# Bringing attention's output back to tokens by DMA transpose instead of TensorE

## The chip, the cores and the metric

The kernel runs on one core of one Trainium2 chip. The metric is the device time of one execution in microseconds. Beside the plain times there is one execution with the hardware profiler on; all durations of instructions come from that one.

## The reference

Two blocks follow each other, all in 32-bit floats. Attention with 8 batches, 8 heads, 576 tokens and head dimension 64, in which each row of scores keeps its 32 largest; then an FNet layer over the 512 channels that the heads give together.

```python
scores = scale * np.matmul(q, k.transpose(0, 1, 3, 2))
kth = np.partition(scores, -top_k, axis=-1)[..., -top_k:-top_k + 1]
scores = np.where(scores >= kth, scores, -1000000000.0)
attn = np.exp(scores - np.max(scores, axis=-1, keepdims=True))
attn = attn / (np.sum(attn, axis=-1, keepdims=True) + 1e-09)
attn_out = np.matmul(attn, v)
...
x = attn_out.transpose(0, 2, 1, 3).reshape(B, S, H * D)
mixed = np.real(np.fft.fft(np.fft.fft(x, axis=1), axis=2))
u = x + mixed
un = (u - mean(u)) / np.sqrt(var(u) + 1e-06)
out = u + np.maximum(un @ w_ch1, 0.0) @ w_ch2
```

`w_ch1` has 512 x 2048 elements, `w_ch2` 2048 x 512.

## The kernel before

**Pairs, items and steps.** Two heads of a batch make a pair: 32 pairs, four for each batch. A pair is cut into 9 items of 128 rows of scores (`IN_PAIR`, L314): eight are 128 queries of one head, the one at position 4 holds the 64 left-over queries of both heads. So there are 288 items, and the main loop (L1468) emits one step for each: step i brings the scores of item i+3, the top-32 search of item i, the masking and exponential of item i-1, and so on. Each engine works through its own list in the order in which the loop emits it; engines meet at semaphores. In the text, "position" is an item's or step's place in its pair, 0 to 8.

**One item.** TensorE makes the scores, ScalarE copies them to SBUF; VectorE finds the 32 largest with four `MAX8` and three `MATCH_REPLACE8` (L406, L408), seven passes over 576 elements for each item; GpSimd turns the first and last of them into the two biases `nt` (`bounds`, L411); ScalarE and GpSimd mask (`mask`, L424), ScalarE takes the exponential with the sum of each row (`expo`, L434). The rows stay unnormalised; the sums go into `den`.

**P to key-major order.** The product with V needs P with keys on partitions. In batch 0, in pair 7 and in the last pair TensorE transposes it (`transposes`, L489). In the 26 other pairs (4 to 30 without 7, `by_dma`, L419) P goes by DMA: `plane` (L445) splits the 32-bit words into planes of low and high 16-bit halves with two ScalarE copies and SyncE writes them to DRAM (step i+2), and `turn` (L472) reads them back with a DMA transpose of 16-bit elements into `PT`, so that the halves come to lie beside each other again (step i+3). All these DMAs are issued on SyncE's queue, in order, with the loads of Q, K and V, the weight parts (`bring`, L884) and the stores of the output.

**The product and the way back to tokens.** A pair's queries form two chunks: chunk 0 has 320 (128, 128 and the 64), chunk 1 has 256. `attend` (L533) makes the output of a chunk in one PSUM bank `o`, with both heads' 64 channels on partitions and queries in the columns; in the 26 pairs it is emitted at the end of the step four after the chunk's last item (`chunk_at`, L1421). `attended` (L551) has ScalarE copy `o` to `xT` in SBUF and prepares the reciprocals `rd` of the row sums. `to_tokens` (L572), one step later, has TensorE transpose `xT` in 128-column pieces (three for chunk 0, two for chunk 1) into the same PSUM bank, and VectorE multiplies the result by `rd` into `x`, the batch's token-major activation: one instruction of 128x256 for each chunk, and one of 64x128 for chunk 0's tail. In batch 1, except for its last chunk, ScalarE does this multiplication in pieces of 64 columns (`normalise_on_act`, L600). `x` has two buffers, so a batch's chunks wait until the batch two before is stored (`written`).

**The FNet layer between.** When all chunks of batch b are in `x`, a plan made ahead (L1356) places the folding of x (GpSimd in the middle batches), the token and channel transforms on TensorE, the statistics and the transposition of u at fixed steps counted from `T0`. At the end the batch's MLP units join a queue (`mlp_units`, L930), and each step takes as many as its planned TensorE time leaves room for (`level`, L1441, spreads the queue up to the next batch's arrival). The last batch's MLP runs after the last step. GpSimd has places in a step: "pool0" is ahead of `bounds`; `some_sums` (L909) puts deferred sums of the MLP into what room is left.

Of the kernel before, what the change touches and what calls it, by code (L numbers as in the profile page):

```python
# [9 lines left out]
F32 = mybir.dt.float32  # L10
I32 = mybir.dt.int32
U32 = mybir.dt.uint32
U16 = mybir.dt.uint16
AF = mybir.ActivationFunctionType
ALU = mybir.AluOpType
# [4 lines left out]
P = 128  # L20
# [53 lines left out]
def kernel(  # L74
# [9 lines left out]
    nc = tc.nc  # L84
# [326 lines left out]
    def bounds(i):  # L411

        if i < N:
# [2 lines left out]
                out=Nt[i], in0=M8.pop(i)[:, 0:TOPK:TOPK - 1], in1=cc, op=ALU.mult  # L416
            )

    def by_dma(i):  # L419

        pair = i // PER_PAIR
        return NPB <= pair < NPAIR - 1 and pair != 2 * NPB - 1

    def mask(i, then=None):  # L424

# [125 lines left out]
    def attended(pair, ch, late):  # L551

        o, w = o_of.pop((pair, ch)), CW[ch]
        PT.pop((pair, ch))
        xT = attp.tile([P, CW[0]], F32, name=f"xT_{pair}_{ch}", tag="xT", bufs=4)
        nc.scalar.copy(out=xT[:, 0:w], in_=o[:, 0:w])
        xT_of[pair, ch] = xT
        den = den_t[pair % 3]
        if ch == 0:
            for h in range(2):  # L560
                nc.scalar.copy(
                    out=den[TH * h:TH * (h + 1), 5:6],
                    in_=den[TAIL + TH * h:TAIL + TH * (h + 1), 4:5],
                )
        c0, n = (0, 6) if ch == 0 else (6, 4)
        rd = small.tile([P, 6], F32, name=f"rd_{pair}_{ch}", tag="rd", bufs=6)

        nc.scalar.activation(out=rd[:, 0:n], in_=den[:, c0:c0 + n], func=AF.Copy, bias=1e-9)
        late.append(lambda: nc.vector.reciprocal(out=rd[:, 0:n], in_=rd[:, 0:n]))
        rd_of[pair, ch] = rd  # L570

    def to_tokens(pair, ch, at_once=True):  # L572

        b, hp = divmod(pair, NPB)
        if b not in x_of:
            x_of[b] = batp.tile([P, 5, DM], F32, name=f"x_{b}", tag="x", bufs=2)
        x = x_of[b]
        xT, rd = xT_of.pop((pair, ch)), rd_of.pop((pair, ch))
        shape, name = [P, 4, P], f"tpx_{pair}_{ch}"
        tp = ps_o.tile(shape, F32, name=name, tag="o") if at_once else bank(shape, name)  # L580
        for n, t in enumerate(CHUNKS[ch]):
            nc.tensor.transpose(tp[0:ROWS[t], n, :], xT[:, P * n:P * n + ROWS[t]], ident)
        cols = slice(P * hp, P * (hp + 1))

        def normalise():
            nc.vector.tensor_tensor(
                out=x[:, 2 * ch:2 * ch + 2, cols].rearrange("p t (e d) -> p t e d", e=2),
                in0=tp[:, 0:2, :].rearrange("p t (e d) -> p t e d", e=2),
                in1=rd[:, 0:4].rearrange("p (t e) -> p t e", e=2).to_broadcast([P, 2, 2, D]),
                op=ALU.mult,  # L590
            )
            if ch == 0:
                nc.vector.tensor_tensor(
                    out=x[0:TAIL, 4, cols].rearrange("p (e d) -> p e d", e=2),
                    in0=tp[0:TAIL, 2, :].rearrange("p (e d) -> p e d", e=2),
                    in1=rd[0:TAIL, 4:6].to_broadcast([TAIL, 2, D]),
                    op=ALU.mult,
                )

        def normalise_on_act():  # L600
            for n, t in enumerate(CHUNKS[ch]):
                r = slice(0, ROWS[t])
                for e in range(2):
                    hd = slice(D * e, D * (e + 1))
                    nc.scalar.mul(
                        out=x[r, t, cols][:, hd], in_=tp[r, n, hd],
                        mul=rd[r, 2 * n + e:2 * n + e + 1],
                    )


        if b == 1 and (hp, ch) != (NPB - 1, 1):
            at(now[0] + 1, "act", normalise_on_act)
        else:
            (late_now if at_once else late_next).append(normalise)
        return 0.14 * len(CHUNKS[ch])
# [662 lines left out]
    def at(step, where, fn, cost=0.0):  # L1278
        plan.setdefault((step, where), []).append(fn)
        costs[step] = costs.get(step, 0.0) + cost  # L1280
# [75 lines left out]
    for b in range(B):  # L1356
        end = PER_BATCH * (b + 1) - 1
        last = b == B - 1
        first, soon = b == 0, b == 1
        T0 = end + (2 if first else 3 if soon else 4 if last else 5)  # L1360
        if first:

            for op in fold_tails(b, nc.gpsimd):
                at(T0 - 1, "pool", op)

            def folds(b=b):
                for par, space in ((0, "own"), (1, "hT")):
                    for op in fold_ops(b, par, nc.vector, space):
                        op()
            at(T0, "dve", folds)  # L1370
            ft, fc = (T0 + 1, T0 + 1), T0 + 1
        elif soon:

            for n, op in enumerate(fold_tails(b, nc.gpsimd)):
                at(T0 - 2 + n, "pool0", op)
            for par in range(2):
                def folds(par=par, b=b, T0=T0):
                    for n, op in enumerate(fold_ops(b, par, nc.gpsimd)):
                        at(T0 + 1 + 3 * par + min(n, 2), "pool0", op)
# [24 lines left out]
        for n, t in enumerate((0, 1, 4, 2, 3)):  # L1404
            quick = first or last
            s = fc + (0 if first else n // 3 if last else n // 2)
            at(s, "pe2", lambda b=b, t=t, q=quick: dft_channels(b, t, q), 1.75)
            if not quick:
                at(s, "pool2", lambda b=b, t=t: add_mixed(b, t))
                at(s + 1, "dve", lambda b=b, t=t: stats(b, t))  # L1410
            at(s + (1 if quick else 2), "pe", lambda b=b, t=t: channels_first(b, t), 0.6)
            if first and t == 4:
                at(s + 1, "pe", lambda: (queue.extend(waiting), waiting.clear()) and 0.0)
        at(s + 1, "begin" if quick else "dve", lambda b=b: rsqrt(b))
        arrivals.append(s + (1 if quick else 2))
        at(arrivals[-1], "units", lambda b=b: (queue if b else waiting).extend(mlp_units(b)))
# [4 lines left out]
    def chunk_at(i):  # L1421

        for tile in (i - 4, i - 3, i - 2):
            r = tile % PER_PAIR
            if PER_BATCH <= tile < N and r in (4, 8):
                if i - tile == (4 if by_dma(tile) else 2 if tile == 2 * PER_BATCH - 1 else 3):
                    return tile // PER_PAIR, r // 8
        return None, None
# [20 lines left out]
    def run(i, where):  # L1449
        for fn in plan.pop((i, where), []):  # L1450
            fn()
# [13 lines left out]
    for op in top_ops(0, (0, 1)):  # L1465
        op()
    i, carry = 0, 0.0
    while i < N + 5 or plan or queue or sums:  # L1468
        now[0] = i
        run(i, "begin")  # L1470
        pair_of = i // PER_PAIR
# [19 lines left out]
        fixed += preps  # L1491

        tok = []

        if pending and pending[0][0] <= i and (
            i < 2 * PER_BATCH + 4 or chunk_at(i)[0] is None
        ):
            _, pp, pc = pending[0]
            if pp // NPB < 2 or pp // NPB - 2 in written:
                pending.pop(0)  # L1500
                tok.append(lambda: to_tokens(pp, pc, not short))
        if not short:
            fixed += tok
        for where in ("pe1", "pe2", "pe"):
# [19 lines left out]
        room = step_us - carry - fixed_cost(i)  # L1524
        cost, got = carry, 0.0
        turn(i - 3)
        if by_dma(i - 1):
            mask(i - 1)
        plane(i - 2, 0)
# [24 lines left out]
        if pair is not None:  # L1554
            cost += attend(pair, ch)
            attended(pair, ch, late_next)
            pending.append((i + 1, pair, ch))
        if i < N:
            if q_step:
                load_nat("k", pair_of + 1)  # L1560
# [67 lines left out]
```

## Time and profile before

| | |
|---|---|
| time, median of 3 runs | 1900.06 us (1898.37 to 1906.79) |
| the profiled execution | 1894.46 us, span 1892.7 us |
| mean granted TensorE clock | 0.953 |
| DMA traffic | 249.19 MB, 50.1% of the 16 engines' time |
| DMA transposes into `PT` | 130, on SyncE's queue |
| `MAX8` and `MATCH_REPLACE8` on VectorE (L406, L408) | 1482 us busy in all |
| steps on GpSimd's clock: first `nt` to last | 17.2 to 1699.1 us |

A row of the group view gives the instruction's line, engine and operation, the tile it writes and those it reads, shapes, the number of instructions, their busy time and mean duration, and then the idle time of the engine just before them with what ended it. Matmul times are those of a pipeline: a single one shows 273 ns where several in a row advance by some 140 ns.

### The profile page before, as it was taken

The page shows a single profiled execution, that of the slowest core. Times are in us where ns is not written, and L with a number is a line of the kernel's source. Part 1 is how long each engine was busy: PE and PEld are TensorE (multiplying, and loading weights), DVE is VectorE, ACT ScalarE, POOL GpSimd, SP SyncE. Part 2 cuts the span into 40 slices and gives each one's busy share as a digit, 9 for nine tenths or more (in the row PEclk, how much of TensorE's full clock was granted, in tenths as well). Part 3 has the DMA queues.
Part 4 walks back from the last instruction along what each step waited for, and adds up shares of the span by engine and source line. Part 5 has one row for each costly group of instructions (what it writes and reads, how often), then busy time and mean ns, then how long its engine had stood idle before and what let it go on. Part 6 is the DMA issues. An engine that isn't in the chain of part 4 may idle for free.

```text
span 1892.7 us, 27288 instructions
## 1 busy us (share of the span) xinstructions
PE 1720.7 (91%) x8134; PEld 1086.8 (57%) x8134; DVE 1580.9 (84%) x3301; ACT 1296.3 (68%) x3104; POOL 911.6 (48%) x1278
## 2 busy tenths in 40 slices
PE   5667699889899999999999999999999999999999
PEld 3344364365456654566456665666556655667677
DVE  7999999699899999997998998998999999862110
ACT  6878658577787777776777687767787778652100
POOL 4768643354745356354643565355544465341012
PEclk8878899899899999999999999999999999999999
DMA  5333026561567755585465854585456755430132
GB/s 166 106 93 108 20 63 167 155 158 32 137 154 191 179 132 131 135 208 141 123 157 135 228 123 124 146 218 145 124 147 172 198 129 144 122 116 6 50 101 80
DMA packets 521972, 249.19 MB, mean 132 GB/s; under 512 B 403680, under 2 KB 511841, under 8 KB 521825
## 3 DMA queue, kind: packets, MB, share of 16 engines
q1 hardware_dynamic: 521040, 247.24, 50.1%
q8 instruction: 65, 1.06, 0.2%
q14 instruction: 83, 0.67, 0.1%
q10 hardware_dynamic: 784, 0.21, 0.0%
HBM read 93.63 MB, written 84.74 MB: 94 GB/s over the span
## 4 chain that ended last, share of the span: by engine, by line
PE 64%; DVE 11%; ACT 9%; DMA 6%; POOL 5%; issue 3%; SPq 2%; POOLq 0%; DVEq 0%; ACTq 0%
PE hp L944 23%; PE cp L971 9%; PE o L542 8%; DVE m L406 5%; PE sp L382 5%; DVE wk L408 5%; PE yp L733 3%; PE cw L1141 3%; PE cv L1141 3%; PE cp L1010 3%; ACT wk L451 2%; POOL wk L430 2%; ACT wk L427 2%; DMA PT<-planes 2%; PE sp_t L352 2%
## 5 line engine op out<-in xcount | busy, mean ns | idle before, releaser
L430 POOL TENSOR_TENSOR wk<-S,wk 128x576 f32<-128x576 f32 x288 | 408.1, 1417 | 570.0 <-ACT wk L427 564.7
L406 DVE MAX8 m<-wk 128x8 f32<-128x576 f32 x864 | 626.7, 750 | 6.0
L944 PE MATMUL hp<-unT,w 128*128 128x256 f32 (+1 forms) x2048 | 533.9, 411 | 3.3 <-ACT hT L948 2.5
L944 PEld LDWEIGHTS hp<-unT,w 128*128 128x128 f32 x2048 | 378.0, 191 | 133.7 <-issue 29.9
L408 DVE MATCH_REPLACE8 wk<-m,wk 128x576 f32<-128x576 f32 x576 | 427.5, 742 | 0.0
L451 ACT COPY wk<-S 128x576 uint16<-128x576 uint16 x468 | 288.7, 666 | 0.1
L427 ACT ACTIVATE wk<-S,nt 128x576 f32<-128x576 f32 x288 | 222.3, 772 | 72.1 <-POOL nt L415 71.1
L971 PE MATMUL cp<-w,hT 128*128 128x512 f32 x512 | 247.8, 621 | 0.0
L406 DVE MAX8 m<-S 128x8 f32<-128x576 f32 x288 | 214.0, 743 | 34.5 <-ACT S L356 34.3
L542 PE MATMUL o<-PT,v 128*64 128x256 f32 (+3 forms) x1440 | 206.4, 430 | 24.9 <-DMA PT<-planes 16.7
L408 DVE MATCH_REPLACE8 wk<-m,S 128x576 f32<-128x576 f32 x288 | 213.6, 742 | 0.0
L438 ACT ACTIVATE S<-wk,nt 128x576 f32<-128x576 f32 x234 | 182.6, 781 | 43.8 <-POOL wk L430 42.6
L948 ACT ACTIVATE hT<-hp 128x320 f32<-128x320 f32 (+1 forms) x256 | 103.6, 410 | 151.5 <-PE hp L944 150.8
L382 PE MATMUL sp<-kT,qT 64*128 64x512 f32 (+1 forms) x528 | 180.3, 680 | 13.1 <-ACT means L1329 5.1
L542 PEld LDWEIGHTS o<-PT,v 128*64 128x64 f32 x1440 | 118.5, 158 | 110.5 <-issue 30.1
L971 PEld LDWEIGHTS cp<-w,hT 128*128 128x128 f32 x512 | 94.1, 197 | 110.4 <-issue 108.6
L385 ACT COPY S<-sp 128x512 f32<-128x512 f32 (+1 forms) x264 | 141.8, 587 | 18.1 <-PE sp L382 17.2
L1086 POOL TENSOR_TENSOR hT<-hT 128x512 f32<-128x512 f32 x64 | 81.4, 1275 | 99.3 <-ACT hT L948 86.4
L415 POOL TENSOR_TENSOR nt<-m,cc 128x2 f32<-128x2 f32 x288 | 58.6, 204 | 117.9 <-DVE m L406 113.9
L352 PE MATMUL sp_t<-kt,qT 128*128 128x128 f32 x320 | 71.9, 308 | 44.8 <-ACT S L374 27.4
L352 PEld LDWEIGHTS sp_t<-kt,qT 128*128 128x128 f32 x320 | 55.6, 197 | 99.2 <-ACT S L374 41.7
L1141 PE MATMUL cw<-w,hT 128*128 128x256 f32 x448 | 105.8, 383 | 0.9 <-issue 0.6
(160 smaller groups left out, 2130.4 us busy)
## 6 DMA issues: line engine op xcount, KB each, us to landing
planes<-wk SPq DMA_DIRECT2D x208, 288.0 KB
w<-w_parts SPq DMA_DIRECT2D x82, 512.0 KB
space<-in_moe_w_ch_dram SPq DMA_DIRECT2D x32, 512.0 KB
nat<-in_q_dram SPq DMA_DIRECT2D x128, 64.0 KB
v<-in_v_dram SPq DMA_DIRECT2D x128, 64.0 KB
out_dram<-x SPq DMA_DIRECT2D x32, 256.0 KB
nat<-in_k_dram SPq DMA_DIRECT2D x124, 64.0 KB
w_parts<-w_t SPq DMA_DIRECT2D x8, 512.0 KB
```

What stands on the lines that cost most here:

```text
L352: nc.tensor.matmul(sp[:, 0:P], lhsT=qT[:, q_end - P:q_end], rhs=kt_t, start=True, stop=True)
L382: nc.tensor.matmul(sp[r], lhsT=qT[hd, q_cols], rhs=kT[hd, :], start=True, stop=True)
L406: ops.append(lambda src=src, m8=m8: nc.vector.max(out=m8, in_=src))
L408: ops.append(lambda src=src, m8=m8: nc.vector.match_replace(w, m8, src, NEG))
L427: nc.scalar.activation(out=w, in_=Ssb[i], func=AF.Relu, scale=-FAR, bias=Nt[i][:, 1:2])
L430: nc.gpsimd.tensor_tensor(out=w, in0=Ssb[i], in1=w, op=ALU.subtract)
L438: nc.scalar.activation(out=Ssb[i] if by_dma(i) else w, in_=w, func=AF.Exp, bias=Nt.pop(i)[:, 0:1], accum_out=den_t[pair % 3][:, c:c + 1],)
L451: nc.scalar.copy(out=words[:, half, :], in_=src[:, half, :])
L542: nc.tensor.matmul(o[D * e:D * (e + 1), c0:c1], lhsT=vv[:, c, e, :], rhs=pt[:, NF if c == NF else (NF + 1) * e + c, c0:c1], start=(c == 0) ...
L944: nc.tensor.matmul(hp[:, 0:w], lhsT=w1[:, dt, P * it:P * (it + 1)], rhs=unT[:, dt, 0:w], start=(dt == 0), stop=(dt == NDT - 1),)
L971: nc.tensor.matmul(cp, lhsT=hT[:, it, P * n:P * (n + 1)], rhs=w2[:, it, :], start=(it == 0), stop=(it == NIT - 1),)
L1141: nc.tensor.matmul(dst, lhsT=h()[a][:, kc, :], rhs=rhs_of(kc), start=start and kc == 0, stop=kc == NK - 1, skip_group_check=True,)
```

## The change

In the 26 pairs whose P goes by DMA, the output of a chunk goes the same way. ScalarE copies `o` out of PSUM twice, as the low and the high 16-bit halves of its words (`words`, in the buffers of `xT`); SyncE writes the two planes to a DRAM tile `oplanes` (one DMA for the 256 columns of full tiles, for chunk 0 a second one for the 64 of the tail). Two steps later, instead of one, `to_tokens` issues a DMA transpose from there straight into `x` (chunk 0: a second one for the tail), in a new place "turn" of the step just behind the one of P. In the step after that GpSimd multiplies by `rd` in place, ahead of `bounds`. TensorE's transposes, the second use of the PSUM bank and the multiplication on VectorE (in batch 1 on ScalarE) go away for these pairs. `T0` of batches 2 to 6 moves from `end + 5` to `end + 7`, and with it everything planned from it.

```diff
+    def pair_by_dma(pair):
+        return NPB <= pair < NPAIR - 1 and pair != 2 * NPB - 1
     def by_dma(i):
-        pair = i // PER_PAIR
-        return NPB <= pair < NPAIR - 1 and pair != 2 * NPB - 1
+        return pair_by_dma(i // PER_PAIR)
...
         o, w = o_of.pop((pair, ch)), CW[ch]
         PT.pop((pair, ch))
-        xT = attp.tile([P, CW[0]], F32, name=f"xT_{pair}_{ch}", tag="xT", bufs=4)
-        nc.scalar.copy(out=xT[:, 0:w], in_=o[:, 0:w])
-        xT_of[pair, ch] = xT
+        if pair_by_dma(pair):
+            words = attp.tile([P, 2, CW[0]], U16, name=f"ow_{pair}_{ch}", tag="xT", bufs=4)
+            src = o[:, 0:w].bitcast(U16).rearrange("p (s h) -> p h s", h=2)
+            for half in range(2):
+                nc.scalar.copy(out=words[:, half, 0:w], in_=src[:, half, :])
+            to = xT_of[pair, ch] = dramp.tile(
+                [P, 2, CW[0]], U16, name=f"oplanes_{pair}_{ch}", tag="oplanes", bufs=6
+            )
+            nc.sync.dma_start(out=to[:, :, TAIL:], in_=words[:, :, 0:2 * P])
+            if ch == 0:
+                nc.sync.dma_start(out=to[:, :, 0:TAIL], in_=words[:, :, 2 * P:])
+        else:
...
         xT, rd = xT_of.pop((pair, ch)), rd_of.pop((pair, ch))
+        cols = slice(P * hp, P * (hp + 1))
+        if pair_by_dma(pair):
+            rows = xT.rearrange("p h s -> (p h) s")
+            nc.sync.dma_start_transpose(
+                out=x[:, 2 * ch:2 * ch + 2, cols].bitcast(U16), in_=rows[:, TAIL:]
+            )
+            if ch == 0:
+                nc.sync.dma_start_transpose(out=x[:, 4:5, cols].bitcast(U16), in_=rows[:, 0:P])
+            def normalise_in_place():
+                for t0, nt, n, r in ((2 * ch, 2, 0, P), (4, 1, 4, TAIL))[:2 - ch]:
+                    xs = x[0:r, t0:t0 + nt, cols].rearrange("p t (e d) -> p t e d", e=2)
+                    by = rd[0:r, n:n + 2 * nt].rearrange("p (t e) -> p t e", e=2)
+                    nc.gpsimd.tensor_tensor(
+                        out=xs, in0=xs, in1=by.to_broadcast([r, nt, 2, D]), op=ALU.mult
+                    )
+            at(now[0] + 1, "pool0", normalise_in_place)
+            return 0.0
...
-        T0 = end + (2 if first else 3 if soon else 4 if last else 5)
+        T0 = end + (2 if first else 3 if soon else 4 if last else 7)
...
-    while i < N + 5 or plan or queue or sums:
+    while i < N + 7 or plan or queue or sums:
...
         if pending and pending[0][0] <= i and (
-            i < 2 * PER_BATCH + 4 or chunk_at(i)[0] is None
+            i < 2 * PER_BATCH + 4 or chunk_at(i)[0] is None or pair_by_dma(pending[0][1])
         ):
...
-                tok.append(lambda: to_tokens(pp, pc, not short))
+                if not pair_by_dma(pp):
+                    tok.append(lambda: to_tokens(pp, pc, not short))
+                else:
+                    at(i, "turn", lambda: to_tokens(pp, pc))
...
         turn(i - 3)
+        run(i, "turn")
...
-            pending.append((i + 1, pair, ch))
+            pending.append((i + (2 if pair_by_dma(pair) else 1), pair, ch))
```

More of the change, by code (lines that the diff above doesn't have):

```diff
@@ L554, in attended @@
         PT.pop((pair, ch))
-        xT = attp.tile([P, CW[0]], F32, name=f"xT_{pair}_{ch}", tag="xT", bufs=4)
-        nc.scalar.copy(out=xT[:, 0:w], in_=o[:, 0:w])
-        xT_of[pair, ch] = xT
+        if pair_by_dma(pair):
[10 more added lines that the diff above has]
+        else:
+            xT = attp.tile([P, CW[0]], F32, name=f"xT_{pair}_{ch}", tag="xT", bufs=4)
+            nc.scalar.copy(out=xT[:, 0:w], in_=o[:, 0:w])
+            xT_of[pair, ch] = xT
         den = den_t[pair % 3]
@@ L582, in to_tokens @@
             nc.tensor.transpose(tp[0:ROWS[t], n, :], xT[:, P * n:P * n + ROWS[t]], ident)
-        cols = slice(P * hp, P * (hp + 1))
         def normalise():
```

## Prediction

> **What bounds the kernel now.** I read first the busy shares and the chain of work that ended last, for the engine to look at.
>
> ```profile
> PE 1720.7 (91%) x8134; PEld 1086.8 (57%) x8134; DVE 1580.9 (84%) x3301; ACT 1296.3 (68%) x3104; POOL 911.6 (48%) x1278
> ...
> PE 64%; DVE 11%; ACT 9%; DMA 6%; POOL 5%; issue 3%; SPq 2%; POOLq 0%; DVEq 0%; ACTq 0%
> ```
>
> TensorE (PE) is busiest and holds two thirds of the chain. That is a mean over stages, so next the busy time by stretch (stretch; length, PE busy, weight loads, DVE, ACT, POOL; clock, DMA share, GB/s).
>
> ```profile
> 500.00:700.00 200.00, 188.20 (x925) 120.46 (x922) 190.61 (x398) 158.63 (x379) 98.48 (x148) 0.97 0.65 163
> ...
> 910.00:1120.00 210.00, 201.97 (x974) 127.16 (x973) 194.65 (x406) 159.00 (x380) 104.71 (x155) 0.98 0.61 156
> 1120.00:1330.00 210.00, 202.02 (x963) 126.72 (x962) 190.50 (x398) 157.99 (x377) 104.56 (x155) 0.97 0.60 154
> 1330.00:1540.00 210.00, 204.23 (x1007) 129.43 (x1006) 195.82 (x409) 160.23 (x385) 106.21 (x157) 0.98 0.63 158
> ```
>
> From 910 us on, PE is 96 to 97% busy and DVE 91 to 93%: PE sets the pace there, DVE has some 15 us in 210 to spare. Before (500 to 700) PE has 94% and DVE 95%: either may set it. ACT (76%) and POOL (50%) have room everywhere. Third, what the way to tokens costs now (minimum/median/maximum ns).
>
> ```profile
> L582 PE MATMUL tpx<-ident,xT x160: 272/273/330, 51.5 to 1724.5; 128*128 128x128 f32 x128, 128*64 128x128 f32 x32
> L586 DVE TENSOR_TENSOR x<-tpx,rd x57: 382/425/426, 56.7 to 1724.8; 128x256 f32<-128x256 f32 x57
> L605 ACT ACTIVATE x<-tpx,rd x36: 305/316/349, 299.1 to 449.0; 128x64 f32<-128x64 f32 x28, 64x64 f32<-64x64 f32 x8
> L593 DVE TENSOR_TENSOR x<-tpx,rd x28: 273/273/275, 57.1 to 1698.5; 64x128 f32<-64x128 f32 x28
> ```
>
> **A, transposes off PE.** Five for each of 26 pairs, 130. In the timeline at 1000 us the three of a chunk 0 take 0.43 us from their start to the next product's start, the two of a chunk 1 at 1004 us 0.22 us: 0.65 a pair, 17 us in all, my lower bound. PE is marked busy with them for 0.49 + 0.38 us, 22.6 us in all, my upper bound. (That the PSUM bank is no longer used twice is worth nothing: products lie four or five steps apart, the second use is over in one.) I take 20, between. Of the 26 pairs 15 (pairs 16 to 30) lie where PE is the bound; I count 95% there. The other 11 lie where PE shares the bound; I count 55%. 20 x (15/26 x 0.95 + 11/26 x 0.55) = 15.6 us. Range 10 (lower bound, a third lost to idle PE) to 22.6.
>
> **B, normalising off DVE.** 23 pairs (batch 1 has it on ACT) x (2 x 0.42 + 0.27) = 25.6 us of DVE. Behind PE it lies hidden, also the 50.6 us in which DVE waited for `tpx`: DVE was ahead and only waited earlier than it would otherwise. In 455 to 860 us, 8 pairs, 8.9 us, DVE is a co-bound: a quarter, 2 us. Range 0 to 6.
>
> **C, ACT.** A second copy out of PSUM for each chunk. The trace has no 16-bit copy from PSUM; the rows nearest are the 32-bit copy of as many elements and the 16-bit strided copy in SBUF.
>
> ```profile
> L556 ACT COPY xT<-o 128x320 f32<-128x320 f32 x32 | 13.7, 428 | 53.5 <-PE o L542 53.5
> L556 ACT COPY xT<-o 128x256 f32<-128x256 f32 x32 | 11.9, 371 | 37.1 <-PE o L542 37.0
> ...
> L451 ACT COPY wk<-S 128x576 uint16<-128x576 uint16 x468 | 288.7, 666 | 0.1
> ...
> L1113 POOL TENSOR_TENSOR x<-x,ct 128x256 f32<-128x256 f32 x30 | 21.6, 729 | 4.5 <-ACT ct L1111 4.3
> ```
>
> By L556 it is 0.43 + 0.37 = 0.80 us a pair, 20.8 us; by L451's 1.16 ns per element 0.67, 17 us. I take 20.8. Batch 1 gives back 30 pieces of 0.32, 9.6 us. Net 11 us on an engine with 24% idle; the copies stand behind the chunk's product, ahead of the next step's work. At ACT's 9% of the chain it is 1 us. Without that cover, 11.
>
> **D, POOL.** 52 multiplications of 128x256 at L1113's 0.73 us and 26 tails of 64x128 (nearest: 128x128 at L629, 0.46) make 50 us. POOL idles 570 us ahead of its mask (the row of L430), waiting for ACT. But the place is ahead of `bounds`: queued behind the multiplication stands `nt`, for which ACT's mask waits. In the timeline POOL is idle 1.1 us between mask and `nt`, so 0.73 fits; chunk 0's 1.19 just does not. I take 1 us; if 1.2 us came on the path in 52 steps it were 62, which needs both PE and DVE without stock, so for the range 8.
>
> **E, SyncE and DMA.** Each pair adds three writes at L464's median 0.56 (1.7 us) and three transposes. A turn of 256 rows x 1152 columns is issued in 2.54 us (median of L484), of half as many rows in 1.26: in proportion, 256x256 takes 0.56, 256x128 0.28. No row has so small a transpose; the bounds are the plain issue's 0.44 and the turn's 1.26. I take 0.6, 0.6 and 0.5: 1.7 us. So 3.4 us a pair, 88 us on SyncE in all. What is queued behind? Loads, planes, turns; and PE's product waits for the last turn. That is tight: product 0 of a pair starts when the last turn has just landed.
>
> ```profile
> 991.40 0.60 SPq L980 DMA_DIRECT2D out_dram<-x  x1
> 997.86 0.54 SPq L464 DMA_DIRECT2D planes<-wk  x1
> 998.45 2.24 SPq L237 DMA_DIRECT2D nat<-in_q_dram  x4
> 1000.79 0.88 SPq L267 DMA_DIRECT2D nat<-in_q_dram  x2
> 1001.77 2.69 SPq L484 DMA_TRANSPOSE PT<-planes  x1
> 1004.56 0.58 SPq L466 DMA_DIRECT2D planes<-wk  x1
> ...
> 1008.38 1.29 SPq L484 DMA_TRANSPOSE PT<-planes  x1
> ```
>
> From 997.86 on the queue runs back to back into the planes of position 4 and its turn at 1008.38; the product starts at 1012.57. But it stood idle from 992.0 to 997.86, waiting for ACT's plane copies. The new transposes come just ahead of that: chunk 1's at position 5, chunk 0's at position 1, both positions without a turn of their own, so 0.6 to 1.1 us fall into this wait.
>
> ```profile
> SPq L464 <- ACT wk L451: 306.9, 104, 15.1
> SPq L484 <- DMA planes<-wk: 193.2, 109, 4.5
> ...
> PE o L542 <- DMA PT<-planes: 16.7, 7, 7.6
> PEld o L542 <- DMA PT<-planes: 9.2, 2, 8.5
> ```
>
> The writes add a wait on SyncE, for ACT's copies after the product. Behind it stands the turn of position 6 (after chunk 0) or 1 (after chunk 1), needed four steps later: about 1 us late, hidden. Not hidden: at a batch's start the chunks that waited for the store come on four successive steps, one perhaps ahead of the planes of position 4: 1 us, six times. The transposes move 26 x 256 x 640 elements more, an eighth of the turns' 26 x 1152 x 1152, at a DMA share of 0.6. I take 2 us; range 0 to 26 (1 us on each of 26 products 0).
>
> A rule speaks against the move. The Trainium skill, "VectorE: DVE Perf Modes", section "Rules for kernel authors", advises TensorE for a 128x128 transpose if the result may lie in PSUM, and the DMA crossbar otherwise; its section "The three transpose paths" gives 390 ns and 1309 ns for bf16. By these, five transposes in two halves would cost 13 us of transfer a pair in place of 2 us on PE, and if they stood on the path the kernel would lose some 290 us (an estimate from that page). The case's rows (0.14 us on PE, 2.5 us issue for a turn) agree on which is dearer; they say nothing against paying with a queue that waits.
>
> **F, the plan.** `T0` two steps later moves the MLP of batches 1 to 5 two steps back: batch 1's is spread over 44 steps instead of 42, and the debt is paid after batch 6's arrival. An MLP's products on PE come to (533.9 + 247.8 + 105.8 + 89.4 + 65.1)/8 = 130 us a batch (L944, L971, L1141 twice, L1010), 3.6 a step: 7.2 us of PE work leave the stretch 530 to 780 us, where PE isn't the only bound, and come back where it is. If 60% is saved there, 3 us are lost. Range 0 to 7.2. The two steps are what `x` comes later by: the transpose one step, the multiplication another; nothing reads `x` before `T0 - 2`.
>
> **Sum.** -15.6 - 2 + 1 + 1 + 2 + 3 = -10.6, about -11 us. The profiled execution (1894.46, of it 1892.7 span) lies 5.6 below the median of the runs shown, so it would come to 1883.5 and the median to 1900.06 - 11 = **1889 us**. Changes under 0.5% (9.5 us) count as none.
>
> **Rivals.**
> 1. PE's freed time becomes idle: DVE needs 7 x 0.745 = 5.2 us a step against 5.8, so it isn't the limit, but ACT and the landing of turns could be. Then a third of A (5 us) and nothing of B remain, less C to F's 7: about 1902, no change. For it: product 0 starts on a landing, so a PE that is earlier waits for it. Against: PE idles only 6 to 8 us in 210.
> 2. The turn becomes the bound (slower): SyncE's 3.4 us more per pair don't fit into the wait ahead of position 5's planes, the planes and turn of position 4 slip, and PE stands at each product 0. The spare there is about 1 us; it decides from a slip of (11 + 9.5)/26 = 0.8 us beyond it. At 1 us: 26 us instead of E's 2, and 5 us of A lost because PE, earlier, only waits: -11 + 24 + 5 = +18, 1918. For: 25.9 us of PE's waits are this one already. Against: the 306.9 us that SyncE waits for ACT.
> 3. POOL holds: the multiplication waits in order for its transpose's landing, with `nt` and the mask behind it. At 1.5 us in 26 of 52 steps +39 - 11, 1928. Against: the transpose is issued a whole step, 5.8 us, earlier.
>
> That the pairs don't take the new path is excluded by the code: the test is that of P's.
>
> **How the numbers follow.** Forecast 48%, rival 1 27%, rival 2 18%, rival 3 7%. The forecast's own range is 1873 (A at 22.6, B at 6, C to F near 1) to 1890. The whole: 1873 to 1918 leaves out 4% below and, above, half of rival 2 and nearly all of rival 3, some 15%. Faster 0.48, same 0.27, slower 0.25.
>
> **What would show it.** Right: 130 fewer PE transposes, PE's share in 910 to 1540 unchanged at 96% or more with shorter steps; POOL near 960 us, ACT near 1307, DVE near 1555; "PE o <- DMA PT" still near 26 us. Rival 1: PE's share falls by 1 to 2 points there. Rival 2: that wait grows over 50 us, and SyncE's wait for ACT shrinks. Rival 3: a wait of POOL's `x` for the new DMA, over 30 us. I am wrong if `T0` costs more than 7 us, seen as a tail after the last `nt` longer than today's 193 us by more than that.

## The result and the profile after

The changed kernel takes 1956.61 us, median of 4 runs (1954.99 to 1960.23); the kernel before took 1899.21 us (1893.26 to 1906.79, 4 runs) beside it. The ratio is 1.0303, 95% interval 1.0263 to 1.0343: 57 us slower, where some 11 us less were predicted and 1918 us was the upper end of the range.

The busy shares and the chain of waits, after:

```profile
PE 1723.6 (88%) x8004; PEld 1085.1 (56%) x8004; DVE 1568.3 (80%) x3232; ACT 1306.2 (67%) x3126; POOL 951.1 (49%) x1356
...
PE 52%; ACT 10%; DMA 10%; DVE 9%; POOL 8%; issue 6%; SPq 4%; POOLq 0%; DVEq 0%; ACTq 0%
```

The 130 transposes are gone from PE (8134 to 8004) and ACT and POOL moved as far as was forecast, DVE half as far; but PE is busy as long as before in a span that is 61 us longer (1953.9 us): 230 us of it are idle, where it was 172. In the chain PE went from 64 to 52% and DMA from 6 to 10%. The stretches of the middle (columns as in the prediction) say the same:

```profile
500.00:700.00 200.00, 175.66 (x842) 113.39 (x841) 181.59 (x373) 153.71 (x369) 94.72 (x147) 0.94 0.68 168
...
910.00:1120.00 210.00, 193.98 (x913) 119.24 (x912) 181.94 (x372) 154.89 (x373) 106.72 (x160) 0.98 0.66 160
1120.00:1330.00 210.00, 194.75 (x910) 121.43 (x911) 184.90 (x379) 155.76 (x371) 109.54 (x165) 0.98 0.67 165
1330.00:1540.00 210.00, 190.25 (x904) 118.62 (x904) 180.91 (x371) 153.39 (x368) 108.03 (x163) 0.97 0.65 158
```

From 910 us on PE is at 91 to 93% instead of 96 to 97%, and DVE at 86 to 88% instead of 91 to 93%: now no engine has a full stretch. What both wait for stands in the waits by engine and line (us in all, times, longest):

```profile
PE o L544 <- DMA PT<-planes: 58.1, 19, 8.6
...
PEld o L544 <- DMA PT<-planes: 23.0, 7, 6.2
...
POOL x L606 <- DMA x<-oplanes: 22.0, 14, 3.9
```

PE's wait for the turn of P has grown from 16.7 us to 58.1. POOL's new wait, 22.0 us in 14 places, is small. On SyncE's own queue, and then the new DMAs one by one (count: minimum/median/maximum ns of the issue, first and last start):

```profile
SPq L466 <- ACT wk L453: 211.4, 58, 14.9
SPq L486 <- DMA planes<-wk: 90.4, 68, 2.0
...
SPq L565 <- ACT rd L582: 73.5, 28, 8.5
...
SPq L565 <- ACT den L575: 68.3, 23, 7.2
...
SPq L596 <- DMA out_dram<-x: 6.8, 4, 1.9
```

```profile
L565 SPq DMA_DIRECT2D oplanes<-ow x52: 533/572/1111, 291.2 to 1728.1; - x52
L596 SPq DMA_TRANSPOSE x<-oplanes x52: 1192/1224/2203, 299.3 to 1733.0; - x52
L567 SPq DMA_DIRECT2D oplanes<-ow x26: 605/606/620, 291.8 to 1702.3; - x26
L600 SPq DMA_TRANSPOSE x<-oplanes x26: 1135/1236/2542, 300.5 to 1707.9; - x26
```

A transpose into `x` holds the queue for 1.22 to 1.24 us whether it is 256x256 or 256x128; 0.6 and 0.5 were assumed. With the writes (52 x 0.57 + 26 x 0.61 = 46 us) the new DMAs take 46 + 78 x 1.23 = 142 us of SyncE instead of the predicted 88. The time in which SyncE stood idle for ACT's planes and for their landing, 500 us before, is down to 302.

The place where this reaches PE is seen in the timeline, SyncE first, then PE (start, us, engine, line), in the second pair of batch 5:

```profile
1211.06 1.23 SPq L596 DMA_TRANSPOSE x<-oplanes  x1
1212.35 1.23 SPq L600 DMA_TRANSPOSE x<-oplanes  x1
1213.69 0.59 SPq L466 DMA_DIRECT2D planes<-wk  x1
1216.31 3.32 SPq L486 DMA_TRANSPOSE PT<-planes  x1
1219.68 1.26 SPq L596 DMA_TRANSPOSE x<-oplanes  x1
```

```profile
1221.95 4.53 PE L544 MATMUL o<-PT,v 128*64 128x256 f32 x20 [5.37 <-DMA PT<-planes]
```

A store issued at 1208.98 us frees `x`, and the chunks that waited for it are brought back on successive steps. SyncE holds the first of their transposes, and with it the queue, until the store has landed (the wait of `L596` for `out_dram` above: 6.8 us in four places, here 1.7). Two transposes stand ahead of the planes, the planes ahead of the turn, and the product of chunk 1 stands 5.4 us for it. From the issue of this store to that of the turn it is 7.3 us; in the kernel without the new DMAs (below) it is 3.6 us at the same place, 1173.52 to 1177.14, and this product doesn't wait. Then the granted clock (windows; the last three columns are clock, DMA share and GB/s):

```profile
1216.50:1221.90 5.40, 0.08 (x1) 0.00 (x0) 5.23 (x15) 3.94 (x11) 1.54 (x2) 0.93 0.84 136
1221.90:1225.30 3.40, 3.35 (x16) 1.95 (x18) 3.40 (x9) 0.00 (x0) 2.20 (x10) 0.50 0.57 145
1225.30:1228.70 3.40, 3.40 (x12) 1.15 (x9) 2.92 (x7) 2.17 (x6) 2.36 (x10) 0.61 0.33 111
1228.70:1232.10 3.40, 3.40 (x15) 2.37 (x14) 3.37 (x9) 1.79 (x4) 1.81 (x4) 1.00 0.97 196
```

After the gap PE runs at half clock for some 6 us (3.4 us at 0.50 and most of the next 3.4): the wait of 5.4 us costs about 3 us more behind it, half of those 6 (an estimate from these rows). That is a second price of every long wait, and the forecast had none.

### The profile page after: what moved, and what is told of

It is laid out like the page before. It is cut to its first block, busy times and chain, and to the rows that moved or that the text cites. A ratio compares the mean times of both kernels' runs of the same rounds, so it can differ in the third digit from the quotient of the medians.

```text
span 1953.9 us, 27252 instructions
## 1 busy us (share of the span) xinstructions
PE 1723.6 (88%) x8004; PEld 1085.1 (56%) x8004; DVE 1568.3 (80%) x3232; ACT 1306.2 (67%) x3126; POOL 951.1 (49%) x1356
## 4 chain that ended last, share of the span: by engine, by line
PE 52%; ACT 10%; DMA 10%; DVE 9%; POOL 8%; issue 6%; SPq 4%; POOLq 0%; DVEq 0%; ACTq 0%
PE hp L976 22%; PE o L544 7%; PE cp L1003 5%; DVE m L406 4%; PE sp L382 4%; DVE wk L408 4%; PE cw L1173 3%; DMA PT<-planes 3%; PE cv L1173 3%; POOL wk L432 3%; DMA planes<-wk 3%; DMA w<-w_parts 3%; ACT wk L429 2%; PE yp L765 2%; ACT wk L453 2%
## 5 line engine op out<-in xcount | busy, mean ns | idle before, releaser
L429 ACT ACTIVATE wk<-S,nt 128x576 f32<-128x576 f32 x288 | 222.4, 772 | 73.8 <-POOL nt L415 73.5
L544 PE MATMUL o<-PT,v 128*64 128x256 f32 (+3 forms) x1440 | 210.8, 440 | 61.9 <-DMA PT<-planes 58.1
L1003 PE MATMUL cp<-w,hT 128*128 128x512 f32 x512 | 242.2, 612 | 0.0
L352 PEld LDWEIGHTS sp_t<-kt,qT 128*128 128x128 f32 x320 | 55.8, 199 | 103.5 <-ACT S L374 41.8
L561 ACT COPY ow<-o 128x320 uint16<-128x320 uint16 (+1 forms) x104 | 36.3, 401 | 96.6 <-PE o L544 96.6
```

The costliest lines, as they stand in the source:

```text
L429: nc.scalar.activation(out=w, in_=Ssb[i], func=AF.Relu, scale=-FAR, bias=Nt[i][:, 1:2])
L544: nc.tensor.matmul(o[D * e:D * (e + 1), c0:c1], lhsT=vv[:, c, e, :], rhs=pt[:, NF if c == NF else (NF + 1) * e + c, c0:c1], start=(c == 0) ...
L1003: nc.tensor.matmul(cp, lhsT=hT[:, it, P * n:P * (n + 1)], rhs=w2[:, it, :], start=(it == 0), stop=(it == NIT - 1),)
```

## The experiments

Ratios are to the kernel before on the same chip, with 95% intervals; "+n us" is the ratio less one, times 1899 us.

**Which part costs the time.** Four kernels take the change apart. The kernel before with only the later `T0` (`t0_alone`):

```diff
-        T0 = end + (2 if first else 3 if soon else 4 if last else 5)
+        T0 = end + (2 if first else 3 if soon else 4 if last else 7)
...
-    while i < N + 5 or plan or queue or sums:
+    while i < N + 7 or plan or queue or sums:
```

> The kernel before with nothing but T0 of batches 2 to 6 at end + 7 (and the loop's end at N + 7). Theory S (SyncE's queue: 78 transposes at 1.2 us of issue and 78 writes that wait for ACT make the turns of P land late) expects the price of my term F alone, 1899 to 1906 us. Theory P (the plan: the folds and transforms now fall on worse positions of the pair, and the MLP comes late) expects most of the 57 us, over 1930.

1921.82 us, ratio 1.0141 (1.0125 to 1.0156): +27 us. And the kernel after with all of its change except the DMAs (`no_dma`; `x` then holds other numbers than attention's output, and that these take the same time is assumed, not shown):

```diff
-            to = xT_of[pair, ch] = dramp.tile(
...
-            nc.sync.dma_start(out=to[:, :, TAIL:], in_=words[:, :, 0:2 * P])
...
+            xT_of[pair, ch] = words
...
-            nc.sync.dma_start_transpose(
...
-                        out=xs, in0=xs, in1=by.to_broadcast([r, nt, 2, D]), op=ALU.mult
+                        out=xs, in0=src, in1=by.to_broadcast([r, nt, 2, D]), op=ALU.mult
```

> The changed kernel without its writes to DRAM and its transposes into x: ScalarE still copies both halves, GpSimd still multiplies, but constants by rd, so x does not hold attention's output. T0 is that of the changed kernel. Theory S expects the loss to be gone: 1885 to 1905 us. Theory P, and a theory L that puts the loss on ScalarE's second copy or on GpSimd's multiplication ahead of the biases, expect it to stay over 1935.

1897.26 us, ratio 1.0009 (0.9992 to 1.0025): +2 us. From here to the kernel after only the writes and transposes are added; the plan is the same step for step, also in the next two. The same kernel with the writes kept (`writes_only`):

> The changed kernel with its writes to DRAM but no transposes into x (GpSimd multiplies constants by rd, x does not hold attention's output). 1897.3 us without both, 1956 with both. If the reads' 1.2 us of issue on SyncE make the loss: 1900 to 1912. If the writes' waits for ScalarE make it: 1935 to 1955. Issuing the writes a step later changed nothing (1958.4), so I expect the former.

1913.14 us, 1.0088 (1.0065 to 1.0110): +17 us. And with the transposes kept, from planes in DRAM that are written once (`reads_only`):

> The changed kernel without its writes: the transposes into x read one fixed DRAM tile, written once at the start, so x does not hold attention's output. If the reads make the loss: 1940 to 1955. If reads and writes share it by their time on SyncE (96 to 46 us): about 1935. If the writes make it: 1900 to 1912.

1931.70 us, 1.0184 (1.0159 to 1.0208): +35 us. So the writes are worth 15 us over the kernel without DMAs, the transposes 33, both 56. The page and the waits of the kernel without the DMAs:

```profile
PE 1696.9 (90%) x8004; PEld 1074.5 (57%) x8004; DVE 1566.2 (83%) x3232; ACT 1303.0 (69%) x3126; POOL 949.3 (50%) x1356
```

```profile
PE o L544 <- DMA PT<-planes: 19.6, 7, 6.7
```

Its span is 1889.7 us; the kernel after's is 64 us longer (the profiled execution without the DMAs was the fastest of its ten, so this is more than the 56 of the ratios). PE's idle time is 193 against 230 us, and the wait for turns alone (19.6 to 58.1) is 38 us. The other 27 us are PE's busy time for the same 8004 instructions (1696.9 to 1723.6). Adding up the granted clock's half-rate stretches over PE's busy time gives a loss of 69 us without the DMAs and 87 with them, so 18 of the 27 are half clock; where the other 9 come from was not followed. With the transposes alone PE's wait for turns is 41.5 us; with the writes alone it is 17.6, no more than without any DMA, so the writes' 15 us come another way, and that was not followed either.

**Does it matter where on the queue they stand?** The new place "turn" moved from behind the turn to behind the planes of item i-2 (`reads_after_planes`):

```diff
         turn(i - 3)
-        run(i, "turn")
         if by_dma(i - 1):
             mask(i - 1)
         plane(i - 2, 0)
...
+        run(i, "turn")
```

> The changed kernel with its transposes into x issued behind the two planes of the step instead of ahead of them. Theory S, if the transposes' place ahead of the planes is what delays the turns: 1920 to 1945 us, and fewer products that wait for a turn (81 us of PE's waits on PT now). If the issue time counts wherever it stands: 1950 to 1960. Theory P: 1957.

1950.64 us, 1.0291 (1.0276 to 1.0306). The writes of `oplanes` issued one step later, where ACT's copies are long done:

```diff
-            nc.sync.dma_start(out=to[:, :, TAIL:], in_=words[:, :, 0:2 * P])
...
+            def write():
+                nc.sync.dma_start(out=to[:, :, TAIL:], in_=words[:, :, 0:2 * P])
...
+            at(now[0] + 1, "turn", write)
```

> The changed kernel with its writes of the planes of o issued one step later, behind the next step's turn, when ScalarE's copies are long done. Theory S, if SyncE's wait for ScalarE at those writes (about 142 us in sum) is what delays the turns: 1920 to 1945 us. If that wait only replaces other idle time of SyncE: 1950 to 1960. Theory P: 1957.

1958.42 us, 1.0330 (1.0314 to 1.0345). The 142 us in which SyncE stood for ACT at the writes fall to 24, its waits for planes and their landing rise from 302 to 402, and the time stays: that wait was idle time SyncE had anyway. Transposes behind the planes and only at the four positions that have no turn of their own, up to two chunks in one step (`reads_free`):

```diff
+            if pair_by_dma(pending[0][1]) and i % PER_PAIR not in (1, 3, 5, 8):
+                break
```

> The changed kernel with its transposes into x issued only at positions 1, 3, 5 and 8 of a pair, which have no turn of their own, behind the planes, two chunks at most at once. If the loss is that the transposes of waiting chunks push the planes and turns of positions 4 to 8: 1920 to 1940. If every microsecond on SyncE counts wherever it stands: 1948 to 1960.

1950.01 us, 1.0324 (1.0270 to 1.0378). PE's wait for turns is 41.8 us in both runs with the transposes moved, instead of 58.1. Of time hardly anything comes of it: by the ratios 2 us less and 4 us more than the kernel after, by the medians 6 and 7 us less. Pair by pair the wait changes its place: PE's gaps at chunk 1's products fall from 38.6 us to 15.4 and 19.3, those at chunk 0's rise from 21.8 to 29.8 and 29.3. So neither of these orders takes the loss away.

**Issue time or traffic?** Plain DMAs of 16 columns, DRAM to DRAM, in place of writes and transposes: two for each transpose, so SyncE is held about as long while almost nothing moves (`issue_only`).

```diff
-            nc.sync.dma_start_transpose(
...
+            for _ in range(4 if ch == 0 else 2):
+                nc.sync.dma_start(out=issue_to[:, :, 0:16], in_=fixed_planes[:, :, 0:16])
```

> Like the run with reads alone (1931.7 us), but each transpose into x is replaced by two small DMAs between DRAM tiles (8 KB each), about the same time of issue on SyncE and hardly any traffic; x is made of constants. 1897.3 us with nothing there. If issue time on SyncE makes the reads' 34 us: 1920 to 1935. If it is the transposes' traffic or GpSimd's wait for their landing: 1897 to 1910.

2027.26 us, 1.0716 (1.0673 to 1.0758). All of them write one DRAM tile, so that each waited for the one before: 195.5 us of waiting on the queue that the transposes don't have. The run is no measure of issue time alone; it shows that waits and issues together cost 134 us over the kernel without DMAs. With 24 tiles in turn instead (`issue_small`):

```diff
+                to = dramp.tile([P, 2, 16], U16, name=f"issue_to_{pair}_{ch}_{_}", tag="issue_to", bufs=24)
+                nc.sync.dma_start(out=to, in_=fixed_planes[:, :, 0:16])
```

> The run with two small DMAs in place of each transpose into x again, but each into a DRAM tile of its own (24 in turn), so that SyncE does not wait for the one before (195 us of such waits in that run). 156 issues of about 0.5 us, 80 us on SyncE, hardly any traffic; x is made of constants, T0 at end + 7. 1897.3 us without them. Theory Q (each microsecond that SyncE's queue is held costs some 0.35 to 0.45 us, whatever holds it: 0.35 with writes or reads alone, 0.41 with both, 0.45 with the waits) expects 1922 to 1935. Theory R (it is the transposes' own: traffic, landing, GpSimd's wait) expects 1897 to 1908.

1920.95 us, 1.0126 (1.0088 to 1.0164): +22 us over the kernel without DMAs (15 to 29 by this run's interval). The DMAs in the view of their tile:

```profile
L592 SPq DMA_DIRECT2D issue_to<-oplanes_fixed x156: 487/605/1454, 298.9 to 1700.1; - x156
```

156 x 0.605 = 94 us of issue, as much as the transposes' 96, cost 22 us where the transposes cost 33. Some two thirds of the transposes' price is thus time on the queue, by the interval from under a half to nearly nine tenths. PE's wait for turns is 33.0 us here. From 500 to 1540 us the medians from issue to landing hardly change between the kernels before and after: 4.68 and 4.74 us for a turn, 2.67 and 2.70 for planes. So the remaining third does not show as slower transfers of these; it stays open.

The other way round, load taken off the queue: the loads of V issued by GpSimd, in the kernel after (`v_pool_after`) and in the kernel before (`v_pool_before`).

```diff
-            load_full(v_of[pair], v, pair)
+            q_of_v = nc.sync if pair == 0 else nc.gpsimd
...
+                for h in range(2):
+                    load_half(v_of[pair], v, pair, e, h, q_of_v)
```

> The changed kernel with the loads of V (6 DMAs a pair, 0.5 us of issue each, 101 us of SyncE in all) issued from GpSimd's queue. Theory Q expects 35 to 45 us less than the 1956 of the changed kernel, 1911 to 1925, less what GpSimd pays for issuing. Theory R expects 1950 or more.

2007.31 us, 1.0591 (1.0555 to 1.0627).

> The kernel before with the loads of V issued from GpSimd's queue. If SyncE's queue already limits the kernel before in the same measure (theory Q without a threshold): 1860 to 1880. If the queue limits only past what it carries there: 1890 to 1905.

1954.96 us, 1.0311 (1.0275 to 1.0348). The edit costs 55 us in the one and 59 in the other, for a reason of its own: in the kernel before with this edit

```profile
L237 POOL DMA_DIRECT2D v<-in_v_dram x124: 720/736/946, 55.5 to 1694.8; - x124
```

an issue takes 0.74 us of GpSimd itself, its busy time rises from 911.6 to 1043.2 us, and ACT's wait for `nt` from 71.1 to 163.5. So the price of a relieved queue can't be read from these times. One thing they do show: in `v_pool_after` SyncE's issues add up to 912 us, against 1016 in the kernel after and 868 without the new DMAs, yet PE waits 62.4 us for turns, as much as before the edit, and 34.2 us at chunk 1's products. The loads of V stand at position 7, those turns at position 2: time taken off the queue in one place is not given back in another.

Last, the weight parts. From batch 1 on the MLP makes chunk 0's second product in seven half-size products instead of eight (`fast`); for these, differences of parts of `w_ch2` are loaded over the weights (T1 to T4), and the parts themselves are loaded back behind them (B12, B21). They belong to the MLP, not to the folding and token transform that the second expectation below names. In the kernel before, T4, T2, T3 and B12 issued one product later (`late_brings`):

```diff
-                    bring(T4, second, part)
+                    bring_held(T4, second, part)
```

> The kernel before with the loads of weight parts (T4, T2, T3, B12) issued one product later, so that SyncE does not stand waiting for the product that still reads the old part (about 60 us of waits in its middle batches). Theory Q without a threshold expects 1870 to 1885; with one 1893 to 1900. If a part comes late for its own product, over 1905.

1891.98 us, 0.9978 (0.9963 to 0.9994): 4 us faster than the kernel before, between the two ranges. The same in the kernel after:

> The kernel after, with the loads of the weights' parts that the folding's and token transform's products issue put one product later on SyncE's queue, as in the run late_brings, where this gave the kernel before 6 us. Nothing is left out of the computation. Theory that SyncE's queue is over a threshold in the kernel after, so that each load moved off a tight place is worth more than in the kernel before: 1935 to 1950. Rival, that what was gained there concerns the weights alone and not the queue: 1948 to 1955, some 6 us below the kernel after at most. If the weights come too late for their products instead: above 1957.

1954.08 us, 1.0299 (1.0271 to 1.0327), 1 us below the kernel after by the ratios. The 6 us or more of the threshold theory did not come. But the test is weak: SyncE's waits for the products ahead of these loads fall only from 132 to 118 us in the kernel before and from 112 to 104 in the kernel after, not by the 60 that were aimed at.

**Why do two steps of `T0` cost 27 us?** `T0` one step later instead of two (`t0_six_alone`):

> The kernel before with T0 of batches 2 to 6 at end + 6. With T0 at end + 7 alone it took 1921.8 against 1896.7 us. Theory C (coincidence: at end + 7 the second half of the token transform, T0 + 11, falls on the step that also ends with a chunk 0's product, position 8; at end + 6 it falls on position 7) expects 1893 to 1904. Theory D (each step of delay costs the same, since the MLP comes later) expects half of the 25 us, 1907 to 1913.

1921.28 us, 1.0120 (1.0089 to 1.0150): +23. One step costs as much as two, so the price is not work pushed back step by step. In the run with two, batches 2 and 3 are 7 us shorter than before, 4 and 5 7 us longer, 6 and 7 16 us longer, and the tail after the last `nt` is 203 us instead of 194. The tail's 10 us are the predicted kind of effect; in the kernel after the tail is 195 us. For the rest, the waits of `t0_alone` against those of the kernel before:

```profile
PE cp L1010 <- DMA w<-w_parts: 19.7, 5, 4.8
```

```profile
PE cp L1010 <- DMA w<-w_parts: 7.2, 2, 6.6
```

L1010 is the MLP's product for the 64 left-over tokens, which needs the parts of `w_ch2` that are loaded back on SyncE's queue. Without the reloads of B12 and B21 (the MLP then computes with what lies there), in the kernel before (`before_no_restore`) and with the later `T0` (`t0_no_restore`):

```diff
-                if ch == 0:
-                    bring(B12, w2_12, part)
...
-                if not last:
-                    bring(B21, second, part)
```

> Control for the next: the kernel before without the four loads a batch that restore parts of w_ch2 (B12, B21) after the seven-product scheme, so the MLP of the following chunks uses wrong weights. TensorE waits 0.6 us for these loads after 860 us. Expected 1888 to 1897, within 0.5% of the kernel before.

1874.63 us, 0.9900 (0.9863 to 0.9938): 19 us less, where at most 0.5% was expected. PE's waits at L1010 for these loads were 7.2 us, so the reloads cost the kernel before more than that wait.

> T0 at end + 7 alone, without the loads that restore B12 and B21 (wrong weights in the MLP). With them it took 1921.8 us, and TensorE's waits for weights (cp on w from w_parts) were 16.1 us after 860 us, against 0.6 in the kernel before. Theory W (T0's price is mostly that these loads now come late in SyncE's queue) expects 1895 to 1906. Theory M (the price is the MLP's work that comes two steps later, and longer steps) expects 1912 to 1922.

1890.51 us, 0.9981 (0.9965 to 0.9997). The price of `T0` falls from 27 to 15 us, so the reloads are some 12 of it (3 to 20 by the intervals). The kernel without DMAs with `T0` at `end + 5`, for which `to_tokens` comes one step earlier and the multiplication in the same step (`no_dma_t0_five`):

> The changed kernel without its DMAs (GpSimd multiplies constants by rd, x does not hold attention's output), with T0 back at end + 5 and the multiplication two steps earlier to fit. It took 1897.3 us at end + 7. If T0's price and what TensorE and VectorE are spared simply add, it loses T0's 25 us: 1868 to 1876. If T0 mattered only because TensorE had to transpose as well, 1890 to 1900.

1913.43 us, 1.0090 (1.0072 to 1.0108): 15 us slower than with `end + 7`, where the kernel before is 27 us faster with `end + 5`. The price of `T0` has no sign of its own. And the kernel before with nothing but a changed account in the planner; the transposes stay (`plan_only`):

```diff
-        return 0.14 * len(CHUNKS[ch])
+        return 0.0 if by_dma(PER_PAIR * pair) else 0.14 * len(CHUNKS[ch])
```

> The kernel before, with only the planner's account changed: in the 26 pairs the transposes are still made and still take their time on TensorE, but the planner no longer counts their 0.14 us per piece. Nothing is left out of the computation. Theory that the time depends on which step the loads of weights and the MLP's units land in (as the 25 us of T0 suggest): 15 us or more away from the kernel before, in either direction. Rival, that the plan's landing is a matter of a few us and T0's price comes from the later start alone: 1894 to 1902.

1922.44 us, 1.0135 (1.0103 to 1.0167): +26 us. Again the reloads are late:

```profile
PE cp L1010 <- DMA w<-w_parts: 23.7, 5, 8.5
```

An account that is 0.42 and 0.28 us off in two steps of a pair moves MLP units and loads to other steps and costs as much as `T0`. This wait is 7.2 us in the kernel before and 6.6 in `no_dma`; in the four kernels with a moved plan and no new DMAs, which are 17 to 27 us slower than the kernel before, it is 14.0 to 23.7. That accounts for 7 to 17 us of each; the rest is spread over many small waits and was not followed further.

## Why the prediction was wrong, point by point

**A and B, off PE and DVE: right in sign; their size was not isolated.** PE's busy time falls by 24 us where the DMAs are left out, but 7 of these are less half clock in that execution (76 us lost before, 69 there); the other 17 are as much as A's lower bound. DVE's falls by 15 us there and by 13 in the kernel after, not by 26, though the 69 multiplications that went away had 25.5 us in their rows; this was not followed. In time, A to D had been summed to -15.6. `t0_alone` to `no_dma` gives -25, but between these two the planner's account changes as well, which alone moved the kernel before by 26. `plan_only` to `no_dma_t0_five`, with one account and one `T0`, gives some -9 by the ratios.

**C and D: right in busy time.** ACT 1306 and POOL 951 us were forecast as 1307 and 960. The multiplication took 0.61 us instead of 0.73, ACT's wait for `nt` behind it went from 71.1 to 73.5 us, and rival 3's sign, over 30 us of waiting for the new DMA, stayed at 22.0.

**E failed, and with it the sign.** It was 2 us, range 0 to 26; measured are 56 (`no_dma` to the kernel after), 54 of the 68 us between forecast and result. Three sentences in it were wrong.

First, the issue of a small transpose, "0.6, 0.6 and 0.5". It was found by proportion from the turn's 2.54 and 1.26, though 1.26, the shortest transpose in the trace, stood there as the other bound. Measured are 1.22 and 1.24: the proportion doesn't go on below 1.26.

Second, that the new issues "fall into this wait". SyncE's idle time before the planes is a sum over 104 waits, not a reserve that can be spent at any point (nor did the queue shown there run back to back: from 1006.44 to 1008.38 it stood for planes to land): 142 us of issue cost 56 us although SyncE still stood idle for over 300 us. The writes alone paid 15 us for 46 us of queue, the transposes 33 for 96, the small DMAs 22 for 94: 0.23 to 0.34 us for each microsecond, and 0.4 for both together.

Third, the place. The danger was looked for at product 0, which "starts when the last turn has just landed". Pair by pair, the start of the product after the landing of its last turn and the longest of PE's gaps at it:

```
                      starts within 0.3 us    median slack    gaps, sum over 26
product 0, before            11 of 26            0.58 us          22.4 us
product 0, without DMAs      12 of 26            0.37 us          19.1 us
product 0, after             12 of 26            0.87 us          21.8 us
product 1, before             1 of 26            4.30 us           0.8 us
product 1, without DMAs       1 of 26            4.05 us           6.7 us
product 1, after             10 of 26            1.74 us          38.6 us
```

Product 0 pays next to nothing more. Product 1 had 4.3 us of slack, was never priced, and pays the waits: the chunks that waited for the store bring their transposes in successive steps in front of its turn. "1 us, six times" saw them, but at position 4's planes and with the wrong size; the waits come once a batch, from batch 2 on, in its second pair, at 2.7 to 5.9 us, and make 27 of the 38.6 us; without the DMAs none of the six is there. (The longest single one, 8.6 us in batch 2's third pair, is there without the DMAs too, with 6.7.) Five of the six are followed by a stretch at half clock, which costs 18 us more in all than without the DMAs.

**F failed, and was given back.** It was 3 us, range 0 to 7.2; alone it is 27 (`t0_alone`). The sign that was named for it, a tail more than 7 us longer, shows in `t0_alone` (10 us) and not in the kernel after (195 us against 194). The step reckoned with PE work moved from a slack stretch to a full one. What moves as well is where each unit and each reload of weights meets SyncE's queue, and the plans tried here lie 15 to 27 us apart: `plan_only` shows it with only the account changed. A to D and F had been summed to -12.6 us; without the new DMAs they come to +2, the other 15 of the 68 us. So F is not what made the kernel slower, but with A to D it took the gain away.

**The rule that was weighed.** The Trainium skill, "VectorE: DVE Perf Modes", section "Rules for kernel authors", advises TensorE where the result may lie in PSUM. The runs agree on the side: the kernel with the DMAs is 56 us slower than the one without. The 290 us that its figures gave did not come: of the transposes' 33 us some two thirds are time on the queue, and the turns and planes beside them landed as fast as before.

**The rivals.** Rival 2 had the mechanism and its sign: PE's wait for turns over 50 us (58.1) and SyncE's wait for ACT shrunk (306.9 to 211.4). Its price of 1 us at product 0 gave 1918; the place was product 1 and the size more than twice that. Rival 1's sign, PE's share down by 1 to 2 points, appeared too (down by 3.5 to 6.7), but by new waits, not because PE's freed time idled. The range left the dear case out at the term itself: with the bound of 1.26 that E names, 26 x (1.7 + 3 x 1.26) are 142 us on SyncE, just what was measured, and that figure was never carried into a time.

## What to carry to other kernels

An in-order queue's idle time is no stock: before adding issues, take for each consumer behind the queue its slack between landing and use, and for the duration of an issue the shortest of its kind in the trace as a floor, not a proportion. Where work is placed by a planner, a change of due times or of one cost moves loads as well as work, so run that change by itself before pricing the rest. And where an engine slows after a gap, price a wait at more than its length.

## What was not expected of the hardware

A DMA transpose of 16-bit elements holds SyncE 1.22 us at 256x256, 1.24 at 256x128 and 1.30 at the turns of 128x1152 (medians in the kernel after); only at 256x1152 is it more, 2.5 to 2.7. Plain DMAs mostly take 0.4 to 0.6 us of SyncE; from GpSimd they take 0.74 us, of an engine that computes. The Trainium skill, "DMA: Bandwidth & Descriptors", section "Rules for kernel authors", says that spreading DMAs over issuing engines only saves the sequencer's issue time; here that time is most of what the transposes cost, and moved to GpSimd it cost 59 us in the kernel before.

After PE gaps the clock was halved as shown above; in the kernel after, every PE gap of over 4 us behind the first 250 us (9 of 9) goes with a stretch of 3.4 to 10 us at 0.50 that begins in the gap and goes on for 3.2 to 6.0 us behind it. The Trainium skill, "TensorE: Matmul & The Clock Gate", section "What's actually happening", gives half rate after an idle window of about 3.4 us; the trace agrees, though some gaps of 1.7 to 3 us were followed by half clock as well.
